# A planner that charges changes of array tiling, a first batch in a newly searched order, and the permutes of batch 2 planned ahead of the output stores

## The chip, the cores and the metric

The kernel runs on one core of a Trainium2 chip. The metric is the device time of one execution in microseconds (us), read as the median of several runs. The time of a run is about 1.7 us longer than the span of its profile (first to last instruction). The span is what the traces are read in.

TensorE is called PE below, VectorE DVE, ScalarE ACT, GpSimd POOL and SyncE SP. "FFN products" are the gate and value matmuls (six matmuls each), "scores" are the query-key matmuls, "values products" multiply the squared scores with v.

## The reference

```python
# q, k, v: (8 batches, 12 heads, 448, 64);  w_gate, w_val: (768, 1536);  w_out: (1536, 768)
scores = scale * np.matmul(q, k.transpose(0, 1, 3, 2))
attn = np.maximum(scores, 0.0) ** 2 / S
attn_out = np.matmul(attn, v)
x = attn_out.transpose(0, 2, 1, 3).reshape(B * S, H * D)      # 3584 x 768
out = (np.maximum(x @ w_gate, 0.0) * (x @ w_val)) @ w_out     # float32
```

## The kernel before

The kernel computes the attention of batch b while the FFN of batch b-1 fills the gaps on PE. It builds a list of operations with guessed durations, and a planner in Python then simulates the engines and fixes the order of instructions on each one. No order is decided on the chip, so a change of the planner's guesses is a change of the program.

```python
class Planner:
    def commit(self, op, s, e):
        op.start, op.eng = s, e
        d = op.engs[e]
        self.t[e] = s + d
        op.end = s + d
        # ... (DMA queue, buffers)

# plan(): which of the two PE streams goes next, attention (A) or FFN (F)
            if att[ai][1] == last_burst:          # inside a burst of scores
                pick = "A" if A[0] <= F[0] + 0.3 else "F"
            elif since >= gap:
                pick = "A" if A[0] <= F[0] + 0.1 else "F"
            else:
                pick = "F" if F[0] <= A[0] + 0.1 else "A"
```

PE works in four tilings of its array, by the shapes of the operands: full 128x128 (FFN, output products, fillers), 64 rows x 128 columns (scores), 64x64 (tail scores, tail of the values products), 128x64 (transposes, values products).

From batch 2 on, q and k are transposed by DMA. DVE first permutes them (seven copies into the buffer `spare`), then SP issues two transposing DMAs. SP's queue also carries the output stores, and it keeps its order.

```python
    def transpose_batch(b):
        # ...
        for s, t in enumerate(slot_order(b)):
            op = Op({"DVE": 0.36}, lambda s=s, t=t: emit_pair(s, t), deps=deps + perm[:1],
                    delay=6.0 if b > 2 else 1.5, alloc=[pair] if s == 0 else [], reads=[st.buf])
        # ...
        for i in range(2):
            op = Op({"SP": 4.5}, lambda i=i: emit_x(i), deps=perm, ...)   # nc.sync.dma_start_transpose
```

The first batch has a hand-given order: `W` are filler matmuls on zeros, `T` transposes, `A0:1` scores of group 0, `VA0` its values product, and a slash lets FFN work in.

```python
    ORDER = ("W1 T0 W2 T1 W2 A0:0f A0:1 W3 A0:2 W4 T2 T3 W2 A1:0 A0:3 W2 A1:1 A1:3 T4 T5 W2 A2:0f ... / "
             "B0:0 VA0f VA1f VA2 B0:1f B0:3 B0:2 / B2:0 B1:0 B1:3 VB0f / B1:1 B2:1f / / / B2:2 B1:2 VB1f B2:3 VB2")
```

## Time and profile before

Before the prediction the time was 439.3 us (median of 3 runs, 438.66 to 439.51).

| what | before | where read |
|---|---|---|
| span | 437.3 us | page, first line |
| PE busy | 428.2 us, 98% | page, part 1 |
| PE waits for the transposing DMA of batch 2 | 0.93 us, at 90.68 us | timeline |
| PE waits for weight block wv_103 | 0.71 us, at 34.39 us | timeline |
| changes of array tiling | 202 | counted in PE's instruction order |

The page of the kernel before; the last line is the chain that ended last, by engine:

```profile
span 437.3 us, 7429 instructions
PE 428.2 (98%) x3026; PEld 224.4 (51%) x3027; DVE 226.9 (52%) x404; ACT 201.7 (46%) x346; POOL 46.8 (11%) x72
...
PE 89%; DMA 8%; POOL 2%; issue 0%; SPq 0%; DVE 0%; ACT 0%; POOLq 0%
```

PE seems the one bound. But its busy time is modelled: the Trainium skill, "Perfetto Trace Analysis", section "Per-engine timelines", says that the profiler estimates the end of a TensorE instruction instead of observing it. So waits have to be looked for one by one. The table of PE's waits of the kernel before (engine, output tile, line, what it waited for: us in total, times, longest):

```profile
PE w_ps L340 <- DVE zeros L753: 1.3, 1, 1.3
PE t_ps L352 <- DMA qk<-in_q_dram: 0.9, 1, 0.9
PE s_ps L475 <- DMA qkT<-spare: 0.9, 1, 0.9
PE v_ps L584 <- DMA wv_103<-in_moe_w_val_dram: 0.7, 1, 0.7
PE s_ps L475 <- ACT r_sb L491: 0.4, 2, 0.2
PE s_ps L481 <- DVE r_sb L493: 0.2, 1, 0.2
```

The wait for qkT in PE's timeline of the kernel before (start, us, engine, line, operation, output and input, shapes, count, and in brackets the idle time before it and its releaser):

```profile
88.46 1.30 PE L584 MATMUL g_ps<-xT,wg_95 128*128 128x448 bf16 x6
90.68 0.74 PE L475 MATMUL s_ps<-qkT 64*128 64x448 bf16 x6 [0.93 <-DMA qkT<-spare]
```

SP's queue just before, in its timeline:

```profile
71.02 6.87 SPq L680 DMA_DIRECT2D out_dram<-o_sb  x4
78.01 10.66 SPq L393 DMA_TRANSPOSE qkT<-spare  x2
88.72 1.29 SPq L680 DMA_DIRECT2D out_dram<-o_sb  x2
```

The transposes were ready to go at 74.83 us, when DVE had ended the permutes (copies from 72.85 us, 1.98 us long), and stood 3.2 us behind the second pair of stores, which waited for their output tile.

### The profile page before, as it was taken

What the parts mean: (1) busy time and instruction counts of PE and PEld (TensorE: products, weight loads), DVE (VectorE), ACT (ScalarE), POOL (GpSimd) and SP (SyncE); (2) the same over time, 40 slices, a digit from 0 to 9 for tenths busy, and PEclk for the clock granted to TensorE, in tenths of its full rate; (3) what the DMA queues carried; (4) which work ended last, traced back from release to release, by engine and by line L of the source; (5) the groups of instructions that cost most, each with busy time, mean ns of one, the idle gap of its engine ahead of it and who ended that gap; (6) DMA issues with size and microseconds to landing.
All of it is one profiled execution on the core that took longest, in us unless ns stands there. A gap on an engine that the chain in (4) does not pass through costs nothing.

```text
span 437.3 us, 7429 instructions
## 1 busy us (share of the span) xinstructions
PE 428.2 (98%) x3026; PEld 224.4 (51%) x3027; DVE 226.9 (52%) x404; ACT 201.7 (46%) x346; POOL 46.8 (11%) x72
## 2 busy tenths in 40 slices
PE   7999999999999999999999999999999999999996
PEld 3577875544454444544455444554445444455553
DVE  2886876176635875484545665553643636102210
ACT  2784565245545555453444444454344444322221
POOL 8535310010002002000200200010000000000000
PEclk9999999999999999999999999999999999999999
DMA  7999999892189655928866990990002200040014
GB/s 107 187 198 199 202 203 192 134 157 36 27 147 197 102 86 77 233 50 117 130 105 109 157 168 1 131 177 1 0 1 73 74 0 1 0 109 0 2 36 108
DMA packets 76706, 44.12 MB, mean 101 GB/s; under 512 B 37632, under 2 KB 73216, under 8 KB 76672
## 3 DMA queue, kind: packets, MB, share of 16 engines
q0 software_dynamic: 39392, 24.38, 39.9%
q1 hardware_dynamic: 37200, 19.17, 22.7%
q8 instruction: 23, 0.38, 0.4%
q14 instruction: 11, 0.09, 0.1%
q10 hardware_dynamic: 80, 0.10, 0.1%
HBM read 48.76 MB, written 11.01 MB: 137 GB/s over the span
## 4 chain that ended last, share of the span: by engine, by line
PE 89%; DMA 8%; POOL 2%; issue 0%; SPq 0%; DVE 0%; ACT 0%; POOLq 0%
PE o_ps L636 26%; PE v_ps L584 24%; PE g_ps L584 24%; PE s_ps L475 7%; PE s_ps L537 6%; DMA wv_103<-in_moe_w_val_dram 3%; DMA wv_100<-in_moe_w_val_dram 2%; DMA qkT<-spare 2%; PE s_ps L481 2%; POOL qk L246 1%; PE s_ps L531 1%; PE t_ps L352 1%; POOL vv L246 0%; SPq L393 0%; POOL wg_94 L246 0%
## 5 line engine op out<-in xcount | busy, mean ns | idle before, releaser
L598 DVE TENSOR_TENSOR hT<-v_ps,g_sb 128x448 bf16<-128x448 f32 (+2 forms) x108 | 61.5, 570 | 109.7 <-PE v_ps L584 109.6
L491 ACT ACTIVATE r_sb<-s_ps 128x448 bf16<-128x448 f32 (+5 forms) x151 | 102.6, 734 | 27.9 <-PE s_ps L475 22.3
L509 DVE TENSOR_TENSOR at<-r_sb 128x896 bf16<-128x896 bf16 (+3 forms) x163 | 93.9, 613 | 28.5 <-ACT r_sb L491 28.2
L591 ACT ACTIVATE g_sb<-g_ps 128x448 bf16<-128x448 f32 (+2 forms) x105 | 53.6, 510 | 118.2 <-PE g_ps L584 112.9
L636 PEld LDWEIGHTS <-hT 128*128 128x128 bf16 x672 | 63.8, 98 | 49.0 <-issue 8.6
L493 DVE TENSOR_SCALAR r_sb<-s_ps 128x896 bf16<-128x896 f32 (+4 forms) x67 | 59.1, 907 | 41.9 <-PE s_ps L475 41.3
L649 ACT ACTIVATE o_sb<-o_ps 128x384 f32<-128x384 f32 (+1 forms) x56 | 27.4, 489 | 69.5 <-PE o_ps L636 69.5
L636 PE MATMUL o_ps<-wo_106,hT 128*128 128x384 bf16 x336 | 59.3, 326 | 0.0
L636 PE MATMUL o_ps<-wo_107,hT 128*128 128x384 bf16 x336 | 59.3, 326 | 0.0
L475 PE MATMUL s_ps<-qkT 64*128 64x448 bf16 (+2 forms) x324 | 37.3, 332 | 1.5 <-DMA qkT<-spare 0.9
L537 PE MATMUL s_ps<-at,vv 128*64 128x448 bf16 x252 | 27.8, 357 | 0.0
L553 ACT CAST xT<-s_ps 128x896 bf16<-128x896 f32 (+2 forms) x23 | 20.1, 874 | 13.8 <-PE s_ps L537 13.8
L475 PEld LDWEIGHTS <-qkT 64*128 64x128 bf16 x324 | 11.8, 94 | 23.2 <-issue 16.0
L537 PEld LDWEIGHTS <-vv 128*64 128x64 bf16 x324 | 15.6, 109 | 14.1 <-issue 7.2
L584 PE MATMUL v_ps<-xT,wv_103 128*128 128x448 bf16 (+2 forms) x108 | 21.2, 332 | 0.7 <-DMA wv_103<-in_moe_w_val_dram 0.7
L584 PE MATMUL g_ps<-xT,wg_94 128*128 128x448 bf16 (+2 forms) x108 | 21.2, 332 | 0.0
L584 PE MATMUL g_ps<-xT,wg_95 128*128 128x448 bf16 (+2 forms) x108 | 21.2, 332 | 0.0
L584 PE MATMUL g_ps<-xT,wg_99 128*128 128x448 bf16 (+2 forms) x108 | 21.2, 332 | 0.0
L584 PE MATMUL v_ps<-xT,wv_101 128*128 128x448 bf16 (+2 forms) x108 | 21.2, 332 | 0.0
L584 PE MATMUL v_ps<-xT,wv_105 128*128 128x448 bf16 (+2 forms) x108 | 21.2, 332 | 0.0
L584 PE MATMUL g_ps<-xT,wg_98 128*128 128x448 bf16 (+2 forms) x108 | 21.2, 332 | 0.0
L584 PE MATMUL v_ps<-xT,wv_102 128*128 128x448 bf16 (+2 forms) x108 | 21.2, 332 | 0.0
(61 smaller groups left out, 336.7 us busy)
## 6 DMA issues: line engine op xcount, KB each, us to landing
out_dram<-o_sb SPq DMA_DIRECT2D x54, 192.0 KB, 2.7
vv<-in_v_dram POOLq DMA_DIRECT2D x14, 384.0 KB, 11.4
qk<-in_k_dram POOLq DMA_DIRECT2D x6, 672.0 KB, 6.4
qk<-in_q_dram POOLq DMA_DIRECT2D x6, 672.0 KB, 9.0
wo_106<-in_moe_w_out_dram POOLq DMA_DIRECT2D x1, 1152.0 KB, 16.8
wo_107<-in_moe_w_out_dram POOLq DMA_DIRECT2D x1, 1152.0 KB, 20.6
qk<-in_k_dram POOLq DMA_DIRECT2D x5, 224.0 KB, 10.8
qk<-in_q_dram POOLq DMA_DIRECT2D x5, 224.0 KB, 9.3
```

The costliest lines, as they stand in the source:

```text
L475: nc.tensor.matmul(half_of(h2)[:, m * n:(m + 1) * n], lhsT=kq(1, j, h2, key_off(b) + c * 128, 128), rhs=kq(0, j, h2, self.c0, n), start=Tr ...
L481: nc.tensor.matmul(half_of(h2)[64 * half:64 * half + 64, :n], lhsT=kq(1, j, h2, key_tail(b), P2), rhs=kq(0, j, h2, self.c0, n), start=True ...
L491: nc.scalar.activation(dst, src, AF.Relu)
L493: nc.vector.tensor_scalar_max(dst, src, 0.0)
L509: lambda: nc.vector.tensor_tensor(self.at_tile(i), loc["r"][:, :2 * ne], loc["r"][:, :2 * ne], ALU.mult),
L537: nc.tensor.matmul(x_of(o, j), lhsT=st.vv[:, 4 * g + 2 * j + h2, 1 + c, :], rhs=self.at(j, c, h2), start=False, stop=(c == NC - 1))
L553: nc.scalar.copy(dst, src)
L584: nc.tensor.matmul(ps, lhsT=w[c][:, kd, o:o + 128], rhs=st.xT[:, kd, cols], start=(kd == 0), stop=(kd == KD - 1))
L591: nc.scalar.activation(loc["gs"], loc["g_ps"], AF.Relu)
L598: nc.vector.tensor_tensor(hs["hT"][:, mf, t0:t0 + n], loc["v_ps"], loc["gs"], ALU.mult)
L636: nc.tensor.matmul(loc["o"], lhsT=hs["hT"][:, kf, ti * 128:(ti + 1) * 128], rhs=w_out_sb[hf][:, kf, :], start=(kf == 0), stop=(kf == KF - 1))
L649: nc.scalar.activation(out=dst, in_=src, func=AF.Copy, scale=float(out_scale))
```

## The change

The intent: the planner adds 0.1 us to its guess whenever PE changes its tiling, so that it would rather merge work of one tiling. The order of the first batch is searched again with that charge. The permutes of batch 2 are planned with 0.3 instead of 1.5 us of delay behind their loads, so that they and the transposes come ahead of more of the output stores. The diff is abridged; "..." and the comments mark the cuts.

```diff
+        self.mode = ("F", "F")          # in Op; ("P","P"), ("S","S"), ("Q","Q"), ("Q","P") set where the op is made
...
     def commit(self, op, s, e):
         d = op.engs[e]
+        if e == "PE":
+            d += 0.1 * (op.mode[0] != self.mode)
+            self.mode = op.mode[1]
         self.t[e] = s + d
...
-        op = Op({"PE": 0.5 if g or b else 0.95}, emit, ...             # transposes
+        op = Op({"PE": 0.45 if g or b else 0.95}, emit, ...
...
-            op = Op({"DVE": 0.36}, ..., delay=6.0 if b > 2 else 1.5,   # permutes
+            op = Op({"DVE": 0.36}, ..., delay=6.0 if b > 2 else 0.3,
...
-            op = Op({"PE": (0.06 if not tail else 0.11) + ne / 2400.0}, emit, ...   # scores
+            op = Op({"PE": 0.02 + ne / 2400.0}, emit, ...
...
-            op = Op({"PE": 0.2 + 7 * n / 2400.0}, emit, ...            # values products
+            op = Op({"PE": 0.15 + 7 * n / 2400.0}, emit, ...
...
-    att.append((Op({"PE": 3.0}, first_zeros), nb))
+    att.append((Op({"PE": 4.8}, first_zeros), nb))
...
-    ORDER = ("W1 T0 W2 T1 W2 A0:0f A0:1 W3 A0:2 W4 T2 T3 W2 A1:0 A0:3 W2 A1:1 A1:3 T4 T5 W2 A2:0f A2:2 A1:2 A2:1f W1 A2:3 / "
-             "B0:0 VA0f VA1f VA2 B0:1f B0:3 B0:2 / B2:0 B1:0 B1:3 VB0f / B1:1 B2:1f / / / B2:2 B1:2 VB1f B2:3 VB2")
+    ORDER = ("W1 T0 W2 T1 W2 A0:0f A0:1 A0:2 W4 T2 T3 A0:3 W1 A1:0 W2 A1:1f T4 T5 A1:3 A2:0f A1:2 A2:2 W2 A2:1f W1 A2:3 B0:0 "
+             "VA0f VA1f VA2 B0:1f B0:3 / B0:2 B2:0f B1:0 B1:3 VB0f B1:1 / / B2:1f B2:2 / B1:2 / / VB1f B2:3 VB2")
```

More of the change, by code (lines that the diff above doesn't have):

```diff
@@ L52, in __init__ @@
         self.landed = []
+        self.mode = "F"
     def ready(self, op):
@@ L363, in transpose_pair @@
         h = 4 * g + 2 * j
-        op = Op({"PE": 0.5 if g or b else 0.95}, emit, deps=list(st.qk_op[h]) + list(st.qk_op[h + 1]) + [id_op],
+        op = Op({"PE": 0.45 if g or b else 0.95}, emit, deps=list(st.qk_op[h]) + list(st.qk_op[h + 1]) + [id_op],
                 alloc=[ps], reads=[st.buf])
+        op.mode = ("P", "P")
         cp = Op({"ACT": 0.84} if b == 0 and g and j == 0 else {"DVE": 0.57, "ACT": 0.84}, emit_copy, deps=[op], alloc=[st.tbuf] if g == 0 and j == 0 else [],
@@ L386, in transpose_batch @@
         for s, t in enumerate(slot_order(b)):
-            op = Op({"DVE": 0.36}, lambda s=s, t=t: emit_pair(s, t), deps=deps + perm[:1], delay=6.0 if b > 2 else 1.5,
+            op = Op({"DVE": 0.36}, lambda s=s, t=t: emit_pair(s, t), deps=deps + perm[:1], delay=6.0 if b > 2 else 0.3,
                     alloc=[pair] if s == 0 else [], reads=[st.buf])
@@ L483, in emit @@
                                          rhs=kq(0, j, h2, self.c0, n), start=True, stop=True)
-            op = Op({"PE": (0.06 if not tail else 0.11) + ne / 2400.0}, emit, deps=[t_op[(b, 2 * g + j)] for j in js],
+            op = Op({"PE": 0.02 + ne / 2400.0}, emit, deps=[t_op[(b, 2 * g + j)] for j in js],
                     alloc=ps + ([self.at_buf] if i == 0 and self.own else []), reads=[st.tbuf])
+            op.mode = ("Q", "Q") if tail else ("S", "S")
             r = Buf(r_r, 1)
@@ L540, in pv @@
             dv = [d for h in range(4 * g, 4 * g + 4) for d in st.v_op[h]]
-            op = Op({"PE": 0.2 + 7 * n / 2400.0}, emit, deps=self.sq + dv, alloc=ps, reads=[self.at_buf, st.vbuf])
+            op = Op({"PE": 0.15 + 7 * n / 2400.0}, emit, deps=self.sq + dv, alloc=ps, reads=[self.at_buf, st.vbuf])
+            op.mode = ("Q", "P")
             def emit_copy(cp, j):
```

## The prediction

> **What bounds the kernel now.** The page gives TensorE 98% of the 437.3 us span (granted clock 0.999), and the chain of waits is 89% PE, 8% DMA. The table of waits finds only about 4.4 us in which PE visibly waits; after 20 us there are two waits that matter: 0.71 us at 34.39 us, where the first value product of weight block wv_103 waits for its DMA, and 0.93 us at 90.68 us, where the first score burst of batch 2 waits for the transposing DMA qkT<-spare. The chain up to 34.4 us is no PE work at all: input DMAs, then wv_100, then wv_103 (issued 20.01, landed 34.34 us). After that it is PE work end to end.
>
> **What the change does, read from the instruction order of both kernels.**
> 1. The charge for array tiling only steers the planner; it costs nothing on the chip. I counted changes of tiling in the PE order: 202 before, 201 after; after the product with wv_103 it is 157 in both. A change costs about 0.10 us in the trace (at 54.2 us a product is followed by a score burst 0.10 us late, and again 0.12 us on the way back). The Trainium skill, "TensorEngine Tiling (Array Packing)", Key Properties, says that changing the tiling mode drains the engine; this agrees. Saved: about 0.1 us, and that before 34 us.
> 2. The first batch's order: four of 27 filler matmuls on zeros go (0.21 us each, estimate from 512 columns in the trace's rate: 0.85 us), one change of tiling goes. The products before the one that needs wv_103 are the same in number, and so is all work after it. The DMA issue order is identical, and that DMA is issued by queue room, not by PE. So I expect PE to come to wv_103 earlier by up to 1 us and to wait longer there: wait 0.7 becomes about 1 to 2 us, gain 0.
> 3. Batch 2: before, SyncE's order is four stores, then two transposes. The seven permutes end at 74.83 us, but the transposes issue at 78.01, behind the stores of the second output tile (stores from 71.02 to 77.9). After: two stores, two transposes, four stores. The permutes still start when the q DMA lands (about 72.8 us); one of the first batch-1 squares now sits between permutes, so they end near 75 to 76 us. The transposes take 12.6 us from first issue to use (78.0 to 90.6), so they land near 88 to 88.6 us. PE would come to the scores at about 89.7 us: the 0.93 us wait vanishes, all on the critical path. The delayed stores cost nothing: three output buffers, the next output tile is at about 116 us.
>
> **Sum.** 439.3 - 0.9 = 438.4 us; rounded down for order effects: 438.3 us. 8 in 10: 437.3 to 439.2. Faster by over 2%: 1%; within 2%: 98%; slower: 1%.
>
> **What would show it.** Waits: qkT<-spare gone from PE's list (step 3); PE's wait for wv_103 longer, start of that product still at 34.4 +- 0.3 us (step 2); busy PE down by about the filler's 0.9 us; transposes issued near 75.5 to 76 us. From 34.4 us to the end, the span should be shorter by 0.9 us and by nothing else.
>
> **What would make it wrong.** Weights landing at other times (then step 2 counts one for one); permutes waiting on VectorE for the q DMA and holding up the square that the last attention-times-values product of batch 1 needs; score bursts packed tighter at the start, with ScalarE and VectorE not emptying PSUM in time, so that PE reaches wv_103 after it landed; a lower clock from fewer filler matmuls.

## The result, and the profile after

Measured: 438.04 us (median of 4 runs, 437.71 to 438.35) against 439.4 us for the kernel before (4 runs, 438.66 to 439.58). The ratio was 0.9972 with a 95% interval of 0.9955 to 0.9989, so the change is clear of the noise and far inside 2%. A later repetition (chip 3) gave 0.9954 (0.9934 to 0.9974). Ratios here are the mean time of one kernel's fast runs over that of the other's in the same rounds, so they are not quite the ratio of the medians quoted beside them.

The page of the changed kernel:

```profile
span 436.2 us, 7424 instructions
PE 427.2 (98%) x3021; PEld 223.9 (51%) x3023; DVE 227.8 (52%) x403; ACT 200.8 (46%) x349; POOL 46.7 (11%) x72
...
PE 91%; DMA 6%; POOL 2%; issue 0%; DVE 0%; ACT 0%; POOLq 0%
```

The span is 1.1 us shorter, and the chain holds 6% of DMA instead of 8%. The table of PE's waits of the changed kernel:

```profile
PE t_ps L357 <- DMA qk<-in_q_dram: 1.5, 2, 1.3
PE w_ps L345 <- DVE zeros L762: 1.3, 1, 1.3
PE v_ps L593 <- DMA wv_103<-in_moe_w_val_dram: 0.7, 1, 0.7
PE s_ps L481 <- ACT qkT L364: 0.6, 1, 0.6
PE v_ps L593 <- DMA wv_102<-in_moe_w_val_dram: 0.3, 1, 0.3
PE w_ps L345 <- issue: 0.2, 1, 0.2
```

The wait for qkT is gone. The sum of the listed waits is not smaller (4.6 us against 4.4), because in the front end PE waits more: 1.5 us for q, 0.6 us for a copy of ACT, 0.3 us for wv_102. All of that lies ahead of 34.3 us, where wv_103 lands anyway. PE's timeline of the changed kernel at batch 2's first scores, and SP's timeline:

```profile
88.30 1.30 PE L593 MATMUL g_ps<-xT,wg_95 128*128 128x448 bf16 x6
89.53 0.74 PE L481 MATMUL s_ps<-qkT 64*128 64x448 bf16 x6
```

```profile
70.09 1.19 SPq L689 DMA_DIRECT2D out_dram<-o_sb  x2
75.96 10.34 SPq L399 DMA_TRANSPOSE qkT<-spare  x2
86.36 2.50 SPq L689 DMA_DIRECT2D out_dram<-o_sb  x4
```

Both traces also tell when the transposes landed: POOL copies one column of qkT as soon as they have. That copy in POOL's timelines of the kernel before and of the changed kernel:

```profile
90.69 0.18 POOL L717 COPY mark<-qkT 64x1 bf16<-64x1 bf16 x1 [32.10 <-DMA qkT<-spare]
```

```profile
88.03 0.18 POOL L726 COPY mark<-qkT 64x1 bf16<-64x1 bf16 x1 [30.79 <-DMA qkT<-spare]
```

The landing moved from 90.69 to 88.03 us, and PE came at 89.53 us, 1.5 us after it.

To see where the rest of the difference lies I cut both traces at one event. It is the start of the first 256-column gate product, which follows the transposes of batch 1's first four heads: 37.77 us before, 37.91 us after. Up to it the kernel is paced by input DMAs ("front end" below). The rest is the same work in both kernels (2600 matmuls in both traces). The spans are taken to 0.01 us from the traces.

| stretch | before | after | difference |
|---|---|---|---|
| front end | 37.77 | 37.91 | +0.14 |
| to the first FFN product behind batch 0's output tiles | 43.88 | 43.58 | -0.30 |
| to batch 2's first scores (7 products in both) | 9.03 | 8.04 | -0.99 |
| to the end | 346.66 | 346.66 | 0.00 |
| span | 437.34 | 436.19 | -1.15 |

The third row is the wait that the prediction was about. The second was not predicted. In PE's timeline of the kernel before, two score bursts stand with a single product between them, ahead of the first output tile:

```profile
63.99 0.74 PE L475 MATMUL s_ps<-qkT 64*128 64x448 bf16 x6
64.67 0.83 PE L584 MATMUL v_ps<-xT,wv_105 128*128 128x256 bf16 x6
65.43 1.04 PE L475 MATMUL s_ps<-qkT 64*128 64x448 bf16 x6
66.39 2.12 PE L636 MATMUL o_ps<-wo_106,hT 128*128 128x384 bf16 x12
```

The first burst takes 0.68 us to the start of what follows (63.99 to 64.67), the second 0.96 us. A burst has three steps of two matmuls, and the weight load of the second burst's last step starts at 66.10 us, 0.31 us after the loads before it. On DVE, the relus of the first burst's scores are these, in its timeline:

```profile
64.42 1.62 DVE L493 TENSOR_SCALAR r_sb<-s_ps 128x448 bf16<-128x448 f32 x2 [0.55 <-PE s_ps L475]
```

They end at 66.04 us. The last step takes one of two pairs of buffers for scores in PSUM (the memory of `s_ps`, which PE writes and DVE and ACT read), and it starts 0.06 us after DVE has emptied one. So the second burst met PSUM that wasn't free yet. The views name no releaser (they put the gap down to "issue"), but the packed trace records which semaphore an instruction waits for: the first matmul of that step waits for number 107, which DVE raises, and the relu that ended at 66.04 us is the only DVE instruction that ended between that step's predecessor (65.79 us) and its start. In the changed kernel two output products stand between the bursts, and both take 0.67 us to the next start:

```profile
64.79 0.74 PE L481 MATMUL s_ps<-qkT 64*128 64x448 bf16 x6
65.46 2.12 PE L645 MATMUL o_ps<-wo_106,hT 128*128 128x384 bf16 x12
67.42 2.11 PE L645 MATMUL o_ps<-wo_107,hT 128*128 128x384 bf16 x12
69.47 0.74 PE L481 MATMUL s_ps<-qkT 64*128 64x448 bf16 x6
70.14 2.12 PE L645 MATMUL o_ps<-wo_106,hT 128*128 128x384 bf16 x12
```

None of this shows in PE's busy time. The windows view of the kernel before for just that stretch (us of the stretch; busy of PE, PEld, DVE, ACT, POOL; clock, DMA share, GB/s) counts PE as fully busy, with the stall inside:

```profile
37.77:81.65 43.88, 43.88 (x421) 29.71 (x418) 29.11 (x59) 23.33 (x42) 8.78 (x12) 1.00 1.26 192
```

### The profile page after: what moved, and what is told of

Its sections match the earlier page's. It is cut to its first block, busy times and chain, and to the rows that moved or that the text cites. A ratio compares the mean times of both kernels' runs of the same rounds, so it can differ in the third digit from the quotient of the medians.

```text
span 436.2 us, 7424 instructions
## 1 busy us (share of the span) xinstructions
PE 427.2 (98%) x3021; PEld 223.9 (51%) x3023; DVE 227.8 (52%) x403; ACT 200.8 (46%) x349; POOL 46.7 (11%) x72
## 4 chain that ended last, share of the span: by engine, by line
PE 91%; DMA 6%; POOL 2%; issue 0%; DVE 0%; ACT 0%; POOLq 0%
PE o_ps L645 26%; PE v_ps L593 25%; PE g_ps L593 25%; PE s_ps L481 6%; PE s_ps L544 6%; DMA wv_103<-in_moe_w_val_dram 3%; DMA vv<-in_v_dram 2%; PE s_ps L487 2%; POOL qk L251 1%; PE s_ps L538 1%; PE t_ps L357 1%; POOL wv_102 L251 0%; POOL wg_97 L251 0%; POOL vv L251 0%; DVE o_sb L660 0%
## 5 line engine op out<-in xcount | busy, mean ns | idle before, releaser
L498 ACT ACTIVATE r_sb<-s_ps 128x448 bf16<-128x448 f32 (+4 forms) x154 | 102.4, 726 | 25.3 <-PE s_ps L481 19.4
L500 DVE TENSOR_SCALAR r_sb<-s_ps 128x896 bf16<-128x896 f32 (+3 forms) x66 | 59.7, 929 | 42.6 <-PE s_ps L481 42.6
```

The lines of the kernel that those rows point to most:

```text
L498: nc.scalar.activation(dst, src, AF.Relu)
L500: nc.vector.tensor_scalar_max(dst, src, 0.0)
```

## The experiments

Theories. **A**: what PE waits at batch 2's first scores is the landing of the transposes minus PE's arrival. SP's order sets the first; the second is set by how many FFN products the planner puts ahead of the scores. **B** (rival): the earlier transposes in SP's order are the gain, by themselves. **C** (rival): a part of the gain comes from the first batch's order at the start of the kernel. The charge as such: a change of tiling costs PE about 0.1 us (theory), or the charge is a fiction (rival).

### The permutes alone

Edit, on the kernel before:

```diff
-            ... delay=6.0 if b > 2 else 1.5,
+            ... delay=6.0 if b > 2 else 0.3,
```

> The kernel before with only the planned delay of batch 2's permutes cut (1.5 to 0.3). SyncE's order becomes two stores, two transposes, four stores, as in the changed kernel, but the planner, which believes the transposes to land early, now puts only 30 FFN matmuls (5 products of 1.135 us) between the last output tile and the first score burst of batch 2, where before has 42. Theory A (PE's wait there is the landing of the transposes minus PE's arrival): transposes issued near 75.5 us, landed near 88.1; PE arrives near 87.4; a wait of about 0.7 us stays, gain only 0.1 to 0.4 us against before. Theory B (the earlier transposes in SyncE's order are the gain): wait gone, gain 0.9 us or more.

Measured: 438.39 us against 439.02 us of before in the same rounds, ratio 0.9995 (0.9978 to 1.0012). In the profile the transposes were issued at 75.74 us and landed at 88.03 us, as early as in the changed kernel, and PE waited all the same, though 0.40 us and not the 0.7 expected. PE's timeline of this kernel:

```profile
86.33 1.30 PE L584 MATMUL g_ps<-xT,wg 128*128 128x448 bf16 x6
88.03 0.74 PE L475 MATMUL s_ps<-qkT 64*128 64x448 bf16 x6 [0.40 <-DMA qkT<-spare]
```

The planner saw the scores ready sooner and put 30 FFN matmuls ahead of them instead of 42. PE came 2.1 us sooner to a DMA that landed 2.7 us sooner. Theory B falls by this trace; the whole times alone leave a gain of up to 0.2% open.

### Charge and order with the old delay of the permutes

Edit, on the changed kernel: `delay` back to 1.5.

> The changed kernel with the old planned delay of the permutes (1.5). SyncE's order goes back to four stores, then the transposes (issue near 78, landing near 90.5 us), but the planner puts 48 FFN matmuls (8 products) before the first score burst of batch 2. Theory A: PE arrives near 90.6 us, so it waits 0 to 0.2 us although the transposes come late; gain 0.7 to 0.9 us against before. Theory B: the wait of 0.9 us is back, gain 0 to 0.2 us.

Measured: 438.4 us, ratio 0.9991 (0.9974 to 1.0008). The profiled run had a late front end (40.03 us to the cut): PE waited 2.32 us for a q of batch 0, then had half the clock from 12.6 to 16.1 us, and waited 0.95 us for the q of batch 1. SP's order was the old one and the transposes landed at 92.65 us, but PE came with 48 FFN matmuls done, at 92.78 us, and no wait is listed. So the wait went without any earlier transpose.

### The charge alone

Edit, on the changed kernel: `ORDER` and the 3.0 us of the first fillers as before, `delay` back to 1.5.

> Only the charge of the planner for changes of array tiling; first batch in the old order, old delay of the permutes. It has 200 changes of tiling (202 before), the two that go lie ahead of the product with wv_103. By the charge alone SyncE's order flips to two stores, transposes, four stores, and 36 FFN matmuls (6 products) come before batch 2's scores. Theory A: landing near 88.1, arrival near 88.5 us, wait 0 to 0.3, gain 0.6 to 0.9 us against before, all of it at batch 2. Rival C (the first batch's order gives a part of the gain): gain smaller than the changed kernel's by that part. A charge that merged anything in the steady part would show as less than 437.3 - 34.4 - 0.9 us from the product with wv_103 to the end; I expect no such thing.

Measured: 438.31 us, ratio 0.9991 (0.9976 to 1.0006). SP's order flipped as read from the build; the transposes landed at 87.37 us, PE came at 88.88 us. The wait is gone, but the two close score bursts are still there (1.10 us from the second's start to the output product, against 0.67), so from the cut to the end it takes 398.71 us, 0.43 us more than the changed kernel.

### The first batch's order alone

Edit, on the kernel before: the new `ORDER` and 4.8 us for the first fillers, no charge, old delay.

> The kernel before with only the new order of the first batch (and the first fillers planned at 4.8 us): no charge, old delay. SyncE: four stores, then transposes; 54 FFN matmuls (9 products) before batch 2's first scores, 201 changes of tiling. Theory A: PE arrives near 91.7 us, after the landing near 90.5: no wait, gain 0.9 us against before. Theory B: no gain. Rival C: gain from the start, PE would reach the product with wv_103 after the DMA landed, or start it earlier than 34.1 us; I expect it at 34.3 +- 0.3 us as in both kernels, since the DMA sets it.

Measured: 438.25 us, ratio 0.999 (0.9974 to 1.0006). Landing at 90.98 us, PE's arrival at 92.38 us with 54 FFN matmuls done, no wait; the close bursts are gone too. The product with wv_103 started at 34.27 us, in the expected place. So rival C is wrong about the place: the order of the first batch pays by what it shifts at 65 and at 90 us, not by an earlier end of the front end.

### Charge and permutes without the new order

Edit, on the changed kernel: `ORDER` and 3.0 us as before.

> The changed kernel with the first batch in the old order: charge and earlier permutes together, without the third part. SyncE's order is two stores, transposes, four stores, but only 24 FFN matmuls (4 products) come before batch 2's first scores. Theory A (PE's wait is the transposes' landing minus PE's arrival): PE arrives 4.54 us after the last output tile, near 86.4 us; the transposes, issued near 75, land 12.3 us later as in the kernel with the permutes only, near 87.3 to 88; a wait of 0.8 to 1.5 us, as long as before's or longer. And the two score bursts with one product between them come back, with the second burst's last step about 0.3 to 0.4 us late for want of a PSUM pair (segment from the first batch-0 products after the transposes of batch 1's second head group to the last output tile: 43.9 to 44.0 us instead of 43.6). Whole time within 0.6 us of before, no gain. Theory B (early permutes are the gain): 0.9 us faster than before.

Measured: 439.67 us against 439.52 us, ratio 0.9996 (0.9976 to 1.0016). No gain. PE's timeline of this kernel at the close bursts and at batch 2's scores:

```profile
66.49 1.17 PE L481 MATMUL s_ps<-qkT 64*128 64x448 bf16 x6
67.59 4.07 PE L645 MATMUL o_ps<-wo,hT 128*128 128x384 bf16 x24
...
88.03 0.74 PE L481 MATMUL s_ps<-qkT 64*128 64x448 bf16 x6 [0.49 <-DMA qkT<-spare]
```

Both losses are back. The wait was 0.49 us and not 0.8 to 1.5, because the front end of this profiled run ended 1.1 us later than before's, which delayed PE and not as much the DMA.

### The changed kernel again

> The changed kernel once more, in the same rounds, to compare. Ratio to before 0.997 to 0.999; profile: no wait for qkT<-spare (0 to 0.3 us), 43.6 us in the segment just named; the front end may differ by 1 us either way with the landing of the q pieces.

Measured in the same rounds as the last one: 437.8 us against 439.52, ratio 0.9954 (0.9934 to 0.9974). No wait for qkT; 43.58 us in the second stretch.

### What these runs say together

From the cut to the end, everything adds up from the two losses. "Stall" is the time from the second of batch 1's last two score bursts to the next product, less 0.67 us.

| kernel | landing | PE at the scores | wait | stall | wait + stall | cut to end |
|---|---|---|---|---|---|---|
| before | 90.69 | 90.68 | 0.93 | 0.29 | 1.22 | 399.57 |
| permutes alone | 88.03 | 88.03 | 0.40 | 0.30 | 0.70 | 399.03 |
| charge + permutes | 88.04 | 88.03 | 0.49 | 0.43 | 0.92 | 399.25 |
| charge alone | 87.37 | 88.88 | 0 | 0.43 | 0.43 | 398.71 |
| charge + order | 92.65 | 92.78 | 0 | 0 | 0 | 398.27 |
| order alone | 90.98 | 92.38 | 0 | 0 | 0 | 398.25 |
| changed kernel | 88.03 | 89.53 | 0 | 0 | 0 | 398.28 |
| changed kernel again | 88.83 | 90.02 | 0 | 0 | 0 | 398.31 |

Each row is one profiled run. In every row the last column is within 0.1 us of 398.3 plus the column before it. For the wait that is theory A, and it is why the parts don't add up as three gains would: each of them moves landing or arrival, and once the wait is 0, moving further brings nothing.

### What a change of tiling costs

Edit, on the changed kernel: the four 64x64 matmuls of the tail come last in a values product, not first. The work is the same, the neighbours are others: 177 changes of tiling from the product with wv_103 on instead of 157. One of the 20 more lies ahead of the cut; from the cut on it is 173 instead of 154.

> The changed kernel with the attention-times-values products in another order: the four 64x64 products of the tail rows last instead of first. Same products, same columns; only the neighbours change: 177 changes of array tiling after the front end instead of 157. What one change of tiling costs is measured by this. Theory: 0.10 us each on PE, so 20 more cost 2.0 us (1.4 to 2.6) from 38 us to the end, and the whole kernel is about 440 us. Rival: the charge is fiction, PE's gaps at changes of tiling have other causes; then 0 to 0.3 us.

Measured: 440.97 us against 439.12 us of before in the same rounds, ratio 1.0038 (1.0017 to 1.0059). From the cut to the end 400.65 us, 2.37 us more than the changed kernel's 398.28, so 0.12 us for each of the 19, and no new wait behind the cut. PE's timeline of the changed kernel and then of this one at a values product behind its tail scores:

```profile
72.19 0.38 PE L487 MATMUL s_ps<-qkT 64*64 64x448 bf16 x4
72.41 0.36 PE L538 MATMUL s_ps<-at,vv 64*64 64x448 bf16 x4
72.70 1.33 PE L544 MATMUL s_ps<-at,vv 128*64 128x448 bf16 x12
73.95 2.12 PE L645 MATMUL o_ps<-wo_107,hT 128*128 128x384 bf16 x12
```

```profile
73.18 0.38 PE L487 MATMUL s_ps<-qkT 64*64 64x448 bf16 x4
73.49 1.32 PE L539 MATMUL s_ps<-at,vv 128*64 128x448 bf16 x12
74.75 0.38 PE L544 MATMUL s_ps<-at,vv 64*64 64x448 bf16 x4
75.06 2.12 PE L645 MATMUL o_ps<-wo,hT 128*128 128x384 bf16 x12
```

From the tail scores to the next product it takes 1.76 us there and 1.88 us here, for the same matmuls with one change more. All 17 such places agree. The three values products that have no tail scores before them keep their number of changes, and they take 1.57 us in both kernels. So the charge of 0.1 us is real.

A second kernel tried to save changes with bursts of four and two score steps:

```diff
-            for k0 in (0, NC):
+            for lo, hi in ((0, 4), (4, 2 * NC)):
                 nb += 1
-                for i in range(k0, k0 + NC):
-                    att.append((pt.s(i, split=i == k0), nb))
-            nb += 1
+                for i in range(lo, hi):
+                    att.append((pt.s(i, split=i < lo + 2), nb))
```

> The changed kernel with score bursts of four and two steps instead of three and three, and the tail and the values products behind them in the same burst: an attempt at fewer changes of tiling. The planner didn't follow: with four PSUM banks shared with the FFN it breaks each burst up, and the order read from the built kernel has 214 changes of tiling after the front end instead of 157. Theory (0.10 us each): 57 more cost about 5.7 us (4 to 8), so about 443.5 us; rival (charge fiction): within 1 us of the changed kernel. A miss on purpose.

Measured: 448.13 us, ratio to before 1.0211 (1.0191 to 1.0231). It was worse than expected. From the cut to the end it took 408.65 us, 10.4 us more than the changed kernel. Its trace lists new waits there: 1.66 us for qkT, 0.78 us for a relu of ACT and 0.60 us for DVE. The 7.3 us left are 0.13 us for each of the 57 changes, near the price above; short stalls inside bursts may be in it, so this kernel supports the price and doesn't measure it.

### Is the front end bound by DMA?

Edit, on the changed kernel: all `W` taken out of `ORDER` (the first eight fillers stay).

> The changed kernel without the 15 filler matmuls after the first eight (3.2 us of PE at 0.213 us each); the first eight stay. Theory (DMA sets the front end up to about 37 us): PE's work up to there gets shorter by about 3 us and the product with wv_103 still starts at 34.3 us +- 0.5, whole time within 0.4 us of the changed kernel (437.7 to 438.5 us), if the granted clock stays at 0.98 or more. Rival (PE's order and fillers bound the front end): 1 to 3 us faster. Third: the fillers keep the clock up; then the clock of the first slices falls below 0.9 and the kernel is slower by a few us.

Measured: 438.22 us, ratio to before 0.9984 (0.9968 to 1.0). The product with wv_103 started at 34.61 us, the cut came at 37.99 us. So 15 fillers less changed nothing measurable, which is what a front end set by DMA should do. (A wait of 0.28 us for qkT was back in this profiled run, and from the cut to the end it took 398.63 us, again 398.3 plus the wait: the margin of the changed kernel isn't a safe one.) But "PE's work gets shorter by about 3 us" was wrong: PE was busy for 28.36 us up to that product, against 29.56 us in the changed kernel. The reason is in the timeline of this kernel and then of the changed one:

```profile
11.37 1.71 PE L357 MATMUL t_ps<-ident,qk 128*64 128x128 bf16 x28 [1.25 <-DMA qk<-in_q_dram]
```

```profile
11.53 0.97 PE L357 MATMUL t_ps<-ident,qk 128*64 128x128 bf16 x28 [1.33 <-DMA qk<-in_q_dram]
```

The same 28 transposes took 1.71 us instead of 0.97. The Trainium skill, "TensorE: Matmul & The Clock Gate", Part 1, says that PE's clock is halved until activity releases it. The traces agree. Their first record of the granted clock, at full speed, starts at 17.5 us without the fillers and at 7.3 us in the changed kernel; the views count the time before it as 1.00, so they don't show this. In the kernel "charge + order", whose trace records half the clock from 12.6 to 16.1 us, 28 transposes took 1.62 us. And four of the six runs without fillers had a mean granted clock of 0.986 to 0.992, where no other run was below 0.994. So the third expectation was right about the clock and wrong about the time: with the fillers, early PE work gets the full clock sooner. Here that is worth nothing in the end, because the DMAs come later still.

A last kernel tried to fill the wait for wv_103. Edit: `VB1f B2:3 VB2` at the end of the order becomes `B2:3 VB1f VB2`.

> The changed kernel with one move in the first batch's order: the tail scores of the last head group go ahead of the values product of the group before, so that both values products are ready before the weight block that PE waits for. Theory: PE's wait of about 0.7 us for wv_103 is filled with a values product that the changed kernel does after it, gain 0.3 to 0.7 us against the changed kernel, unless the next DMA in line (the q of batch 1, which PE meets about 2 us later and which landed near 37 us) takes it over; then gain 0 to 0.2 us and a longer wait for that q. I think the second the more likely by 60 to 40.

Measured: 438.63 us, ratio to before 0.9991 (0.9972 to 1.0009), no better than the changed kernel. In the profile the wait for wv_103 is gone (that product starts at 34.31 us) and PE waits 0.88 us for the q of batch 1 at 36.35 us instead. The next DMA in line took it over, as the second of the two expectations said. No version beats the changed kernel.

### What stays open

The whole-time ratios don't separate the parts: each part's interval includes 1, so what is said of the parts rests on one trace each. "Order alone" and the changed kernel take the same time from the cut to the end (398.25 and 398.28 us), yet their ratios to before were 0.999 on chip 12 for the one, and 0.9972 (chip not on record) and 0.9954 on chip 3 for the other. The traces say where the spread comes from: the front end. The cut lay between 37.77 us (before) and 40.03 us (charge + order) in the profiled runs of these kernels, although the loads of the front end are issued in the same order in all of them. Whether the changed kernel's front end is also a little better on average isn't settled; taking the cut-to-end time off the median spans gives 38.1 and 37.8 us for its two measurements and 37.8 to 38.3 us for the kernel before.

## Why the prediction was right

The prediction was 438.3 us; measured were 438.04 us, inside the range. The wait and its size were right (0.93 us foreseen, 0.99 us in the stretch). That the whole came out so near is in part luck: a stall of 0.30 us went that nobody had seen, and 0.28 us were lost between wv_103 and the cut.

- **The charge finds nothing to merge.** Right: 157 changes of tiling from the product with wv_103 to the end in both kernels, and the last 346.66 us agree within 0.01 us. Three bursts of scores a head group are set by the list of bursts, and the planner can only choose what goes between them. The price was right too (0.12 us measured for 0.10 read). The Trainium skill's page "TensorEngine Tiling (Array Packing)" (Key Properties) says only that there is a drain.
- **Nothing is gained in the front end.** Right in the sum (34.25 against 34.39 us for the product with wv_103, then 37.91 against 37.77 at the cut). The step "wait 0.7 becomes about 1 to 2 us" was wrong: the wait for wv_103 stayed 0.69 us. PE had lost the saved time earlier, in new waits for q (1.5 us instead of 0.9), for an ACT copy (0.6) and for wv_102 (0.25).
- **The transposes come earlier and the wait of 0.93 us goes.** Right in each number: issue 75.96 us (predicted 75 to 76), landing 88.03 (88 to 88.6), PE's arrival 89.53 (about 89.7).
- **"Shorter by 0.9 us and by nothing else" from 34.4 us on** was wrong as put. From the product with wv_103 to the end the trace is 1.01 us shorter, but that is a sum: -0.99 for the wait, -0.30 for a stall inside a score burst (on PSUM) that I had not seen, and +0.28 in the front end between wv_103 and the cut; the rest is 0.00. PE's busy time fell by 1.0 us, as forecast (0.9 us), but 0.37 us of that lie behind the cut, where the stall had counted as busy. In the front end, batch 1's transposes started 0.26 us later after the values product than before (0.94 us behind its start against 0.68), about when the q load that they need landed; POOL, waiting for the same load, went on 0.15 us later.
- **What the prediction took for granted** was that 42 FFN matmuls stand ahead of the scores. That held for the two kernels compared, and it hid that earlier permutes alone would have been answered by the planner with only 30 or 24. The change worked because the new order shifted PE's arrival as well. So the split among the parts was wrong: the prediction gave the first batch's order no gain and the charge 0.1 us, but from the cut to the end the order alone takes 1.32 us off the kernel before and the charge alone 0.86 us, and the earlier permutes alone, which were to bring the whole 0.9 us, 0.54 us.

## What to carry to other kernels

A wait is the difference of two times, and a planner that is told of an earlier landing will move the consumer up by what it believes, so check the built order for both ends before crediting a change. Parts of a change that all shrink one wait don't add up: make the table of landing and arrival for each part alone. Cut traces at a common event behind the noisy front end; there, 0.1 us was readable, while whole times on the chip scattered by 1 us and more.

## What the Trainium skill lacked or had wrong

- "TensorEngine Tiling (Array Packing)", Key Properties: it names the drain at a change of tiling mode but no cost. Here it was 0.10 to 0.12 us (19 more changes cost 2.37 us). At 157 changes that is an estimated 16 to 19 us of this kernel, far more than the whole change brought.
- "TensorE: Matmul & The Clock Gate", Part 1: nothing wrong seen. The run without fillers shows slow early matmuls (1.71 against 0.97 us for 28 transposes), and its first record of the full clock comes at 17.5 us instead of 7.3 us. A mean clock that counts the time before the first record as full hides this (1.00 in that run's profile).
- "Perfetto Trace Analysis", Per-engine timelines: what it says of modelled ends is right, and a consequence could be added: a PSUM stall inside a burst (0.29 us here) counts as busy, 43.88 of 43.88 us, and shows only as the distance to the next start.
